# Doubling the third unit's inverse blocks for all chunks at once, inside the second unit's steps

## The chip, the cores and the metric

The kernel runs on one core of a Trainium2 chip. The metric is the device time of one execution in microseconds. TensorE does the matmuls, VectorE (DVE), ScalarE (ACT) and GpSimd (POOL) the elementwise work, and SyncE (SP) issues most DMAs. Each engine works through its own queue in order and waits for semaphores.

## The reference

Three layers follow each other. The first is linear attention with the delta rule, over 4 batches, 8 heads, 768 positions and 48 dimensions; the second is a gated layer, the third a choice of one of 8 experts for each token.

```python
for t in range(S):
    kt, vt, bt = (k_n[:, :, t], v[:, :, t], beta[:, :, t, None])
    y[:, :, t] = np.einsum('bhd,bhde->bhe', q[:, :, t], state)
    v_old = np.einsum('bhde,bhd->bhe', state, kt)
    state = state + bt[:, :, :, None] * np.einsum('bhd,bhe->bhde', kt, vt - v_old)
...
gate = 1.0 / (1.0 + np.exp(-(x @ w_gate)))
val = x @ w_val
return (gate * val @ w_out).astype(np.float32)
...
e_idx = np.argmax(logits, axis=1)
for e in range(E):
    mask = e_idx == e
    h = np.maximum(xc[mask] @ w1[e], 0.0)
    y[mask] = gate_w[mask, None] * (h @ w2[e])
out[do_compute] = xc + y
```

## The kernel before, in words

The 3072 tokens are cut into 12 units of 256 tokens, u = 0 to 11; the text calls u = 0 the first unit, u = 1 the second, u = 2 the third, u = 3 the fourth. A unit holds four chunks of 64 positions, one for each batch, with 8 heads each.

**Attention.** Inside a chunk the recurrence is a triangular system of 64 x 64 for each head. `gram` multiplies keys with keys and queries (TensorE), and ScalarE copies the products to g (lines 257 and 258) and to the masked query part kq (line 280, then a mask on GpSimd, line 281). From g comes the inverse tt of the system. There are two ways to it:
- The first three units (0 to 2) invert diagonal blocks of 16 on VectorE (`solve16`) and then double them twice with small matmuls: from 16 to 32 and from 32 to 64. That is `spread` (three VectorE instructions for each chunk) and `double` with its products ip, iy, jp and jy. The results of one product are copied by ScalarE or VectorE before the next.
- The units from the fourth on send g through DRAM (scr_g) to a block layout bt (`blocks`), and VectorE solves blocks of 32 in a long row of small instructions (`solve`): norms first (lines 324 to 336), then bt times a factor (340), 31 pairs of a product and a sum (351 and 356), a last product (358). The answer goes back through DRAM to tt, and `combine` finishes it with two products in the unit before its use.

`chain` carries the state through the chunks of a unit: ks at step 3, w at step 5 (it needs tt), y and s at step 7. It makes the input x of the next unit of the gated layer.

**Gated layer.** A unit has twelve steps f = 0 to 11, one for each 128 of the 1536 inner columns. In a step TensorE does the group gv_f (18 matmuls, `first`), ScalarE the sigmoid, VectorE the product sg_f, ScalarE its rounding gh_f and GpSimd the rest gl_f (`gate`); two steps later TensorE adds the step to the accumulators (`second`, lines 849 and 852). gv has two banks in PSUM, so gv_f waits until sg_(f-2) is done. From the second unit on the queues of TensorE, VectorE and ScalarE keep the order in which the program is written (`in_order`). The first unit (`block`) is left to a scheduler with priorities; there the weights are decoded too, and `fold` adds ten columns to each weight tile (transposes at line 775, products at line 781).

**Order around the change.** Behind the first unit the program writes `doubles()`, the third unit's doubling, chunk by chunk in pairs; its priority lets the scheduler put it into the first unit's tail. Then the second unit begins. In its step GRAMF = 0 it writes the fourth unit's grams and blocks and starts that unit's `solve`, a generator that yields an estimated time before each piece; `spend` runs pieces up to a budget for each step (the list SPEND). What is left of a solve when the next unit's grams come is run then. Routing of the unit before (`route`: copies of the accumulators at line 865, nine small VectorE instructions, a rank product) starts in step 0 of the second unit, in step 1 of the others.

The tile yc of the doubling lies in the same memory as the squares of `solve` (tag dn), so the squares wait for the last product jy.

Of the kernel before, what the change touches and what calls it, by code (L numbers as in the profile page):

```python
# [10 lines left out]
F32 = mybir.dt.float32  # L11
# [80 lines left out]
RANKF = 3  # L92
GRAMF = 0
LOADF = 8
LAG = 2
JOINF = 3
WHEN = {5: 1, 7: 4}
SPEND = 0, 0, 1.1, 2.8, 3.6, 4.0, 2.4, 1.2, 2.4, 2.4, 2.4, 2.4


class Kernel:
# [74 lines left out]
def sl(a, n):  # L176
    return slice(a, a + n)


class Attention:  # L180
# [295 lines left out]
    def double(self, u, c, pool, tag, bufs):  # L476

        k, nc = self.k, self.k.nc
        d = self.u[u]
        g, tt, yc, zc, gm = (d[x] for x in ("g", "tt", "yc", "zc", "gm"))  # L480
        s = sl(4 * c, 4)
        rc = d["rc"][:, s]
        quarters = [(pr, 4 * c + pr, slice(q, q + 32), (q, q)) for pr in range(4) for q in range(0, 128, 32)]

        def bank(n, w):
            return pool.tile([128, 4, w], F32, name=f"{n}{u}_{c}", tag=tag, bufs=bufs)

        ps = bank("ip", 16)
        for pr, n, q, at in quarters:
            nc.tensor.matmul(ps[q, pr], gm[q, n], yc[q, n, 16:32], start=True, stop=True, tile_position=at)  # L490
        yield
        nc.scalar.activation(rc, ps, AF.Copy, scale=-1.0)
        ps = bank("iy", 16)
        for pr, n, q, at in quarters:
            nc.tensor.matmul(ps[q, pr], zc[q, n], rc[q, pr], start=True, stop=True, tile_position=at)
        yield
        nc.vector.tensor_tensor(yc[:, s, 16:32], yc[:, s, 16:32], ps, op=ALU.add)
        for b in (1, 0):
            nc.vector.tensor_scalar(tt[:, c, :, sl(32 * b, 32)], yc[:, s], self.sel[:, 6 + b:7 + b], None, op0=ALU.mult)
        nc.vector.transpose(zc[:, s], yc[:, s])  # L500
        ps = bank("jp", 32)
        for pr in range(4):
            for p0 in (0, 64):
                nc.tensor.matmul(
                    ps[p0:p0 + 32, pr], g[p0 + 32:p0 + 64, c, pr, 0:32], tt[p0 + 32:p0 + 64, c, pr, 32:64],
                    start=True, stop=True, tile_position=(p0 + 32, p0))
        yield
        for p0 in (0, 64):
            nc.scalar.activation(yc[p0:p0 + 32, s], ps[p0:p0 + 32], AF.Copy, scale=-1.0)
        ps = bank("jy", 32)  # L510
        for pr in range(4):
            for p0 in (0, 64):
                nc.tensor.matmul(
                    ps[p0:p0 + 32, pr], zc[p0:p0 + 32, 4 * c + pr], yc[p0:p0 + 32, 4 * c + pr],
                    start=True, stop=True, tile_position=(p0, p0))
        yield
        for p0 in (0, 64):
            nc.scalar.activation(tt[p0:p0 + 32, c, :, 32:64], ps[p0:p0 + 32], AF.Copy)
        yield

    def lengthen(self, u, i):
# [726 lines left out]
def turns(*gens, fill={}):  # L1248

    n, more = 0, True  # L1250
    while more:
        more = [1 for g in gens if next(g, g) is not g]
        for f in fill.get(n, ()):
            f()
        n += 1


def program(ctx, tc, io, out):
# [219 lines left out]
        yield  # L1478
        yield from at.solve16(2, 0)

    def doubles():
        banks = (k.ps_a, "rw", 1), (k.ps_a, "y", 1)
        for cs in ((0, 1), (2, 3)):
            for c in cs:
                at.spread(2, c)
            turns(*[at.double(2, c, *banks[c % 2]) for c in cs])

    def between():

        tags = "prep", "rw", "y"  # L1490
# [73 lines left out]
        block()  # L1564
    dctx.close()
    m1.late = k.pool("late")
    with k.band("prep"):
        doubles()
    def spend(pieces, time):

        pieces[1] += time
        with k.band("solve"):
            while pieces[1] > 0:
                pieces[1] -= pieces[2]
                pieces[2] = next(pieces[0], 99)
# [6 lines left out]
    def second():  # L1582
        with k.band("second"):
            m1.second(*behind.popleft())
# [3 lines left out]
    with k.in_order(*engines[0:3]):  # L1588
        for u in range(1, NU):
            more = u + 1 < NU  # L1590
            if more:
                with k.band("top"):
                    xs[u + 1] = xp.tile([128, 2, KT3, UT], F32R, name=f"x{u + 1}", tag="x", bufs=2)
                chain = at.chain(u + 1, xs[u + 1], "prep")
            join = at.combine(u + 1) if 2 < u + 1 < NU else iter(())
            route = m1.route(u - 1)
            for f in range(NF):
                with k.band("main"):
                    fp = m1.first(u, f, xs[u])
                with k.band("gate"):  # L1600
                    g = m1.gate(*fp)
                    q = next(g)
                    drain(g)
                if f == RANKF:
                    with k.band("route"):
                        drain(route)
                if f == GRAMF:
                    spend(solve, 99)
                if f == GRAMF and u + 2 < NU:
                    with k.band("prep"):  # L1610
                        for c in range(CPU_):
                            at.gram(u + 2, c, (k.ps_a, ("prep", "y", "rw", "s")[c], 1))
                        at.blocks(u + 2)
                    solve = [at.solve(u + 2), 0, 1.1]
                if f == JOINF - 1:
                    with k.band("prep"):
                        next(join, None)
                spend(solve, SPEND[f])
                if more:
                    if f == JOINF:  # L1620
                        with k.band("prep"):
                            next(join, None)
                        with k.band("top"):
                            next(chain)
                    if f == JOINF + 1:
                        with k.band("prep"):
                            drain(join)
                    if f in WHEN:
                        with k.band("top"):
                            for _ in range(WHEN[f]):  # L1630
                                next(chain, None)
                    if f == LOADF and u + 3 < NU:
                        load(u + 3)
                    if f == LOADF and 2 < u + 2 < NU:
                        with k.band("prep"):
                            at.beside(u + 2)
                behind.append(q)
                if len(behind) > LAG:
                    second()
                if f == (LAG - 1 if u > 1 else 0):  # L1640
                    with k.band("route"):
                        next(route)
                        next(route)
            if u + 2 == NU:
                at.ctx.close()
                m2 = Moe2(k, m1)
        while behind:
            second()
# [114 lines left out]
```

## Time and profile before

| what | value |
|---|---|
| time, median of 3 runs | 975.41 us (975.26 to 978.01) |
| profiled execution | 984.58 us, of it span 982.8 us |
| TensorE busy | 890.0 us, 91% of the span |
| VectorE busy | 632.5 us, 64% |
| ScalarE busy | 426.1 us, 43% |
| GpSimd busy | 346.1 us, 35% |

The profile is of one execution, and its times count from the span's start. Busy time is the union of an engine's instructions; a line such as "203.54 5.39 PE ... x48" gives the start, the time that the instructions took together, and their number, and in brackets the idle time before them with what ended it. The granted clock is a share of 2.4 GHz: 1.00 is that level, 0.50 is 1.2 GHz, and a value between them is a mix of both in the stretch. In the trace gv_3 of the second unit starts at 216.31, its gv_5 at 225.05, and gv_0 of the third unit at 253.85.

### The profile page before, as it was taken

The numbers are of one execution on the slowest core, as the hardware profiler recorded it, in microseconds if no ns is written. First come the engines' busy times: TensorE is split into PE (matmuls) and PEld (weight loads), VectorE is DVE, ScalarE is ACT, GpSimd is POOL, SyncE is SP. The second block draws the span as 40 slices with busy tenths as digits, with TensorE's granted clock in tenths as the row PEclk, the third lists the DMA queues.
The fourth block names the chain that finished last, engine by engine and source line by source line (L and its number), as shares of the span: only waits on it lengthen the run. The fifth ranks groups of instructions, "written<-read, shape, count | busy, mean of one in ns | idle before, by whom it ended". The sixth has DMA issues, their size and how long they took to land.

```text
span 982.8 us, 26579 instructions
## 1 busy us (share of the span) xinstructions
PE 890.0 (91%) x10833; PEld 852.5 (87%) x10833; DVE 632.5 (64%) x1858; ACT 426.1 (43%) x998; POOL 346.1 (35%) x411
## 2 busy tenths in 40 slices
PE   6259887889999899999999999999989987999996
PEld 5247776789989899898989999898989987999996
DVE  6828886529586675858667575857721234877774
ACT  6365564452444425343442434343223233555553
POOL 6202662342533415253341514343222333231421
PEclk9998878879999999999999999999979999999999
DMA  8490304132313334331333433133020167766620
GB/s 194 143 382 24 76 2 124 31 71 66 82 38 80 94 74 98 78 70 38 85 94 74 98 80 97 40 67 80 10 55 15 34 216 257 223 229 201 222 83 14
DMA packets 132428, 99.29 MB, mean 101 GB/s; under 512 B 88231, under 2 KB 111868, under 8 KB 132304
## 3 DMA queue, kind: packets, MB, share of 16 engines
q1 hardware_dynamic: 125264, 78.44, 29.4%
q0 software_dynamic: 6624, 18.81, 6.4%
q8 instruction: 86, 1.41, 0.7%
q14 instruction: 38, 0.31, 0.1%
q10 hardware_dynamic: 416, 0.33, 0.1%
HBM read 76.66 MB, written 18.61 MB: 97 GB/s over the span
## 4 chain that ended last, share of the span: by engine, by line
PE 63%; DVE 17%; DMA 6%; ACT 5%; issue 5%; SPq 2%; POOL 1%; POOLq 0%; ACTq 0%; DVEq 0%
PE gv L826 24%; PE acc L849 9%; PE poe L1032 6%; PE he L1015 6%; PE acc L852 4%; PE gram L252 3%; PE w L664 2%; PE y L677 2%; DMA raw<-in_w 2%; DVE dec L756 2%; PE s L694 2%; DVE dec L757 1%; DVE sg L837 1%; PE m1p L559 1%; ACT tt L574 1%
## 5 line engine op out<-in xcount | busy, mean ns | idle before, releaser
L826 PE MATMUL gv<-x,w 128*128 128x256 f32 x2592 | 348.7, 289 | 2.2 <-ACT w L765 1.3
L826 PEld LDWEIGHTS gv<-x,w 128*128 128x128 f32 x2592 | 340.0, 196 | 4.2 <-ACT w L765 1.5
L840 POOL TENSOR_TENSOR gl<-sg,gh 128x256 fp32r<-128x256 f32 x144 | 117.1, 813 | 379.8 <-ACT gh L839 361.9
L837 DVE TENSOR_TENSOR sg<-sg,gv 128x256 f32<-128x256 f32 x144 | 60.1, 417 | 131.6 <-ACT sg L836 131.6
L849 PE MATMUL acc<-w,gh 128*128 128x394 f32 x576 | 140.1, 364 | 5.1 <-ACT w L783 3.6
L836 ACT ACTIVATE sg<-gv 128x256 f32<-128x256 f32 x144 | 54.9, 381 | 181.5 <-PE gv L826 178.5
L839 ACT ACTIVATE gh<-sg 128x256 fp32r<-128x256 f32 x144 | 60.2, 418 | 146.6 <-DVE sg L837 146.0
L849 PEld LDWEIGHTS acc<-w,gh 128*128 128x128 f32 x576 | 99.6, 195 | 9.8 <-ACT w L783 3.7
L351 DVE TENSOR_TENSOR tmp<-xx,bt 128x126 f32<-128x126 f32 (+28 forms) x299 | 91.9, 313 | 6.5
L356 DVE TENSOR_TENSOR xx<-xx,tmp 128x126 f32<-128x126 f32 (+28 forms) x299 | 88.3, 301 | 8.9
L281 POOL TENSOR_TENSOR kq<-kq,consts 64x256 f32<-64x256 f32 x96 | 72.9, 759 | 28.7 <-ACT kq L280 19.1
L852 PE MATMUL acc<-w,gl 128*128 128x394 f32 x288 | 78.4, 353 | 3.5 <-POOL gl L840 3.2
L934 DVE TENSOR_TENSOR w2le<-rawe,w2he 128x768 fp32r<-128x768 f32 x66 | 63.4, 962 | 10.1 <-ACT w2he L933 9.4
L252 PE MATMUL gram<-kq 48*64 48x128 f32 x768 | 56.6, 305 | 9.8 <-DMA kq<-in_kq 7.3
L252 PEld LDWEIGHTS gram<-kq 48*64 48x64 f32 x768 | 50.6, 153 | 13.7 <-DMA kq<-in_kq 6.0
L852 PEld LDWEIGHTS acc<-w,gl 128*128 128x128 f32 x288 | 54.9, 195 | 3.6 <-POOL gl L840 3.5
L933 ACT ACTIVATE w2he<-rawe 128x768 fp32r<-128x768 f32 x66 | 55.4, 840 | 2.0 <-DMA rawe<-in_w 1.9
L766 POOL TENSOR_TENSOR w<-dec,w 128x576 fp32r<-128x576 f32 x24 | 32.0, 1348 | 59.7 <-ACT w L765 48.1
L1015 PE MATMUL he<-x2he,w2he 128*128 128x256 f32 x168 | 48.3, 288 | 0.5 <-DVE hle L1024 0.5
L1015 PE MATMUL he<-x2le,w2he 128*128 128x256 f32 x168 | 47.3, 282 | 0.0
L1023 ACT ACTIVATE hhe<-he 128x256 fp32r<-128x256 f32 x64 | 24.5, 383 | 52.5 <-PE he L1015 52.4
L1015 PE MATMUL he<-x2he,w2le 128*128 128x256 f32 x168 | 47.1, 280 | 0.0
(330 smaller groups left out, 1553.5 us busy)
## 6 DMA issues: line engine op xcount, KB each, us to landing
rawe<-in_w SPq DMA_DIRECT2D x64, 384.0 KB, 4.8
raw<-in_w SPq DMA_DIRECT2D x24, 576.0 KB, 7.8
kq<-in_kq SPq DMA_DIRECT2D x44, 192.0 KB, 4.7
kv<-in_kv SPq DMA_DIRECT2D x22, 384.0 KB, 5.3
xa<-x POOLq DMA_DIRECT2D x12, 392.0 KB, 5.9
out<-x POOLq DMA_DIRECT2D x24, 192.0 KB, 4.1
bt<-scr_g SPq DMA_DIRECT2D x18, 256.0 KB, 4.9
xx<-in_eye SPq DMA_DIRECT2D x9, 256.0 KB, 5.4
```

Of the source, the lines that this page charges most:

```text
L252: self.last = nc.tensor.matmul(ps[o0:o0 + 64, pr], kt[r0:r0 + 48, cc, pr, :], kq[r0:r0 + 48, cc, pr, par:par + 2], start=True, stop=True).ins
L281: nc.gpsimd.tensor_tensor(q, q, mask[p], op=ALU.mult)
L351: v.tensor_tensor(t, x[:, :ni, m:m + 1].to_broadcast([128, ni, b - a]), bt[:, m:m + 1, m + 1 + a:m + 1 + b].to_broadcast([128, ni, b - a]) ...
L356: v.tensor_tensor(x[:, :ni, m + 1 + a:m + 1 + b], x[:, :ni, m + 1 + a:m + 1 + b], t, op=ALU.add)
L826: nc.tensor.matmul(gv[:, j], self.part(f, j, w)[:, c], y[:, a], start=n == 0, stop=n == 8)
L837: nc.vector.tensor_tensor(sg, sg, gv[:, 1], op=ALU.mult)
L839: nc.scalar.activation(gh, sg, AF.Copy)
L840: (nc.gpsimd if u < PG else nc.vector).tensor_tensor(gl, sg, gh, op=ALU.subtract)
L849: nc.tensor.matmul(self.acc[t], a[:, s], self.part(f, 2, b), start=f == 0 and n == 0, stop=False)
L852: nc.tensor.matmul(self.acc[t], gl[:, sl(128 * t, 128)], self.part(f, 2, 1), start=False, stop=f == NF - 1)
L934: nc.vector.tensor_tensor(l, raw, h, op=ALU.subtract)
L1015: nc.tensor.matmul(ps, ww[:, 0, s], xx[:, a], start=n == 0, stop=n == 8)
```

## The change

`doubles()` is gone. The third unit's doubling is written into the second unit's steps 1 to 4: in step 1 `spread_all` and the product ip, in step 2 iy, in step 3 jp, in step 4 jy, each for all four chunks in one bank, with the copies behind it merged. The products are as many as before. The fourth unit's grams, their blocks and the start of its solve go from step 0 to step 4 of the second unit, and its solve has a budget list of its own. From the third unit on nothing in the program text differs.

```diff
+GRAMF1 = 4
+DOUBLE2 = 1
 SPEND = 0, 0, 1.1, 2.8, 3.6, 4.0, 2.4, 1.2, 2.4, 2.4, 2.4, 2.4
+SPEND1 = 0, 0, 0, 0, 1.1, 3.6, 4.0, 4.0, 4.0, 2.8, 2.8, 2.8
...
+    def spread_all(self, u):
+
+        v = self.k.nc.vector
+        d = self.u[u]
+        for b in range(2):
+            v.tensor_tensor(
+                d["yc"][:, :, sl(16 * b, 16)], d["td"],
+                d[f"g{b}"].rearrange("p (n o) -> p n o", o=1).to_broadcast([128, 4 * CPU_, 16]), op=ALU.mult)
+        v.transpose(d["zc"], d["yc"])
+
+    def double_all(self, u, pool, tag, bufs):
...
+        def bank(n, w):
+            return pool.tile([128, 4 * CPU_, w], F32, name=f"{n}{u}", tag=tag, bufs=bufs)
+
+        ps = bank("ip", 16)
+        for n, q, at in quarters:
+            nc.tensor.matmul(ps[q, n], gm[q, n], yc[q, n, 16:32], start=True, stop=True, tile_position=at)
+        nc.scalar.activation(rc, ps, AF.Copy, scale=-1.0)
+        yield
+        ps = bank("iy", 16)
+        for n, q, at in quarters:
+            nc.tensor.matmul(ps[q, n], zc[q, n], rc[q, n], start=True, stop=True, tile_position=at)
+        nc.vector.tensor_tensor(yc[:, :, 16:32], yc[:, :, 16:32], ps, op=ALU.add)
+        for b in (1, 0):
+            nc.vector.tensor_scalar(tn[:, :, sl(32 * b, 32)], yc, self.sel[:, 6 + b:7 + b], None, op0=ALU.mult)
+        nc.vector.transpose(zc, yc)
+        yield
+        ps = bank("jp", 32)
...
+        for p0 in (0, 64):
+            nc.scalar.activation(yc[p0:p0 + 32], ps[p0:p0 + 32], AF.Copy, scale=-1.0)
+        yield
+        ps = bank("jy", 32)
...
+        for p0 in (0, 64):
+            nc.scalar.activation(tn[p0:p0 + 32, :, 32:64], ps[p0:p0 + 32], AF.Copy)
+        yield
...
-    with k.band("prep"):
-        doubles()
...
+            grams, budget = (GRAMF, SPEND) if u > 1 else (GRAMF1, SPEND1)
...
-                if f == GRAMF:
+                if f == grams:
                     spend(solve, 99)
-                if f == GRAMF and u + 2 < NU:
+                if f == grams and u + 2 < NU:
...
-                spend(solve, SPEND[f])
+                spend(solve, budget[f])
...
                 if len(behind) > LAG:
                     second()
+                if u == 1 and DOUBLE2 <= f < DOUBLE2 + 4:
+                    with k.band("prep"):
+                        if f == DOUBLE2:
+                            at.spread_all(2)
+                            double = at.double_all(2, k.ps_a, "prep", 1)
+                        next(double)
```

The order of the queues shows where this lands. First TensorE's queue from the first unit's last accumulating group on (acc with gh_11 and gl_11), before the change; jp and jy are the doubling of chunks 2 and 3, gram_1 to gram_3 the fourth unit's grams, gv_1 to gv_3 groups of the second unit.

```order
L849 MATMUL acc_0_1141<-w_2082,gh_11_2150 128x394
L849 MATMUL acc_1_1142<-w_2082,gh_11_2150 128x394
L852 MATMUL acc_0_1141<-w_2082,gl_11_2151 128x394
L852 MATMUL acc_1_1142<-w_2082,gl_11_2151 128x394
L504 MATMUL jp_2_2380<-tt_81,g_1220 32x32 x8
L504 MATMUL jp_3_2393<-tt_81,g_1220 32x32 x8
L513 MATMUL jy_2_2404<-early_y,early_z 32x32 x8
L513 MATMUL jy_3_2415<-early_y,early_z 32x32 x8
L252 MATMUL gram_1_2477<-kq_101 64x128 x8
L252 MATMUL gram_2_2492<-kq_105 64x128 x8
L252 MATMUL gram_3_2507<-kq_105 64x128 x8
L826 MATMUL gv_1_2554<-x_1583,w_850 128x256 x18
```

The same place of the same queue with the change; ip and iy are the doubling of all four chunks.

```order
L903 MATMUL acc_0_1141<-w_2082,gh_11_2150 128x394
L903 MATMUL acc_1_1142<-w_2082,gh_11_2150 128x394
L906 MATMUL acc_0_1141<-w_2082,gl_11_2151 128x394
L906 MATMUL acc_1_1142<-w_2082,gl_11_2151 128x394
L548 MATMUL ip_2256<-early_y,early_bt 32x16 x64
L880 MATMUL gv_2_2322<-x_1583,w_876 128x256 x18
L903 MATMUL acc_0_2348<-w_325,gh_0_2199 128x394 x2
L903 MATMUL acc_1_2349<-w_325,gh_0_2199 128x394 x2
L906 MATMUL acc_0_2348<-w_325,gl_0_2200 128x394
L906 MATMUL acc_1_2349<-w_325,gl_0_2200 128x394
L553 MATMUL iy_2356<-early_bt,early_z 32x16 x64
L880 MATMUL gv_3_2425<-x_1583,w_1181 128x256 x18
```

gv_1 has moved ahead into the tail, the grams are gone from here, and ip stands directly between the tail and gv_2. The next piece is VectorE's queue with the change, from the end of the first unit's routing (oh, ob) to the spread that ip needs and to sg_2.

```order
L937 TENSOR_TENSOR oh_2212<-eq_2211,mx_2210 128x16
L938 TENSOR_TENSOR oh_2212<-oh_2212,cm_2214 128x16
L939 CAST ob_2213<-oh_2212 128x16
L891 TENSOR_TENSOR sg_1_2246<-sg_1_2246,gv_1_2227 128x256
L529 TENSOR_TENSOR early_y<-early_bt,early_nt 128x16x16
L529 TENSOR_TENSOR early_y<-early_bt,early_w 128x16x16
L532 STREAM_TRANSPOSE early_z<-early_y 128x512
L891 TENSOR_TENSOR sg_2_2341<-sg_2_2341,gv_2_2322 128x256
```

The spreads (the two products into early_y) stood in the first unit before, around its sg_10, and stand behind the routing and sg_1 now. The last piece is ScalarE's queue with the change, from the last gram's copies in step 4 to the copies of w in step 5.

```order
L260 ACTIVATE g_2574<-gram_3_2620 64x256
L261 ACTIVATE g_2574<-gram_3_2620 64x256
L283 ACTIVATE kq_105<-gram_3_2620 64x4x64 x2
L327 ACTIVATE sq_0_2650<-kv_102 128x384
L327 ACTIVATE sq_1_2653<-kv_106 128x384
L572 ACTIVATE tt_81<-jy_2662 32x16x32 x2
L890 ACTIVATE sg_5_2716<-gv_5_2697 128x256
L893 ACTIVATE gh_5_2717<-sg_5_2716 128x256
L722 ACTIVATE sw_83<-w_0_2743 64x384
```

The copies of tt were ahead of the grams 1 to 3 and stand behind all grams' copies and behind the two squares now, and the sigmoid of step 5 behind them.

## Rows read from the trace of the kernel before

**Rows 1.** Busy time by stage: stretch, length, PE, PEld, DVE, ACT, POOL, clock, DMA.

```profile
183.20:197.50 14.30, 14.30 (x395) 13.04 (x395) 4.84 (x20) 6.59 (x23) 3.81 (x5) 1.00 0.01 3
197.50:208.86 11.36, 8.84 (x134) 7.74 (x133) 1.50 (x7) 6.46 (x20) 3.44 (x6) 0.75 0.01 2
208.86:216.31 7.45, 7.45 (x44) 7.45 (x43) 2.24 (x11) 3.47 (x10) 5.42 (x8) 0.69 0.69 127
216.31:225.05 8.74, 8.74 (x119) 8.62 (x118) 6.42 (x25) 2.54 (x6) 4.41 (x6) 1.00 0.25 91
220.99:252.48 31.49, 31.49 (x382) 30.92 (x381) 29.57 (x133) 7.79 (x21) 8.79 (x10) 1.00 0.26 59
```

**Rows 2.** Chain that ended last, in the first unit's tail: start, us, what.

```profile
187.35 2.13 PE gv L826 x18
190.11 0.77 PE wt L781 x6
193.40 0.48 PE wt L775 x3
193.87 0.71 PE acc L849 x4
194.58 0.36 PE acc L852 x2
194.94 0.66 PE ip L490 x54
```

**Rows 3.** Timeline of TensorE: fourth unit's grams, then fifth unit's: start, us, what.

```profile
203.54 5.39 PE L252 MATMUL gram<-kq 48*64 48x128 f32 x48 [2.00 <-ACT tt L518]
256.08 3.71 PE L252 MATMUL gram<-kq 48*64 48x128 f32 x64
```

**Rows 4.** Timeline of ScalarE and VectorE: first unit's routing, from its first to last instruction.

```profile
210.46 0.87 ACT L865 ACTIVATE x<-acc 128x394 f32<-128x394 f32 x2
212.78 0.17 DVE L885 CAST ob<-oh 128x16 bf16<-128x16 f32 x1
```

**Rows 5.** Groups by line and shape, VectorE, 218 to 256: busy us, mean ns, idle.

```profile
L837 DVE TENSOR_TENSOR sg<-sg,gv 128x256 f32<-128x256 f32 x9 | 3.7, 416 | 0.3 <-ACT sg L836 0.2
```

**Rows 6.** Timeline of TensorE: gv_3 and gv_5 of the second unit, gv_0 of the third.

```profile
216.31 2.29 PE L826 MATMUL gv<-x,w 128*128 128x256 f32 x18
225.05 2.28 PE L826 MATMUL gv<-x,w 128*128 128x256 f32 x18
253.85 2.29 PE L826 MATMUL gv<-x,w 128*128 128x256 f32 x18
```

**Rows 7.** Timeline of ScalarE: squares in the second unit; copies in the third.

```profile
217.76 0.53 ACT L324 ACTIVATE sq<-kv 128x384 f32<-128x384 f32 x1 [0.62 <-DVE nt L325]
262.73 0.38 ACT L258 ACTIVATE g<-gram 64x256 f32<-64x256 f32 x1
263.13 0.78 ACT L280 ACTIVATE kq<-gram 64x256 f32<-64x256 f32 x2
281.68 1.18 ACT L574 ACTIVATE tt<-x2p 32x512 f32<-32x512 f32 x2
```

**Rows 8.** The blocks' DMAs in the third unit: timeline of SP, then time to landing.

```profile
266.68 1.14 SPq L296 DMA_DIRECT2D bt<-scr_g  x2
DMA to landing us min/median/max: 3.7/4.1/4.6
```

**Rows 9.** Timeline of VectorE in the second unit: key products' subtraction, and sg_10.

```profile
225.97 1.01 DVE L655 TENSOR_TENSOR kv<-kv,ks 128x384 f32<-128x384 f32 x2
252.06 0.41 DVE L837 TENSOR_TENSOR sg<-sg,gv 128x256 f32<-128x256 f32 x1
```

**Rows 10.** A wait at w of a later unit, and the stretch behind it.

```profile
453.50 0.31 PE L664 MATMUL w<-kv,tt 64*64 64x48 f32 x2 [1.45 <-ACT tt L574]
455.70:459.20 3.50, 3.50 (x26) 3.41 (x22) 3.19 (x12) 2.37 (x5) 0.77 (x1) 0.51 0.00 0
```

**Rows 11.** Copies of jy to tt, all doublings: ns min, median, max, first and last start.

```profile
L518 ACT ACTIVATE tt<-jy x24: 250/268/271, 58.5 to 203.2; 32x128 f32<-32x128 f32 x24
```

More of the change, by code (lines that the diff above doesn't have):

```diff
@@ L518, in double @@
             nc.scalar.activation(tt[p0:p0 + 32, c, :, 32:64], ps[p0:p0 + 32], AF.Copy)
+        yield
[8 more added lines that the diff above has]
+    def double_all(self, u, pool, tag, bufs):
+        k, nc = self.k, self.k.nc
+        d = self.u[u]
+        g, tt, yc, zc, gm, rc = (d[x] for x in ("g", "tt", "yc", "zc", "gm", "rc"))
+        quarters = [(n, slice(q, q + 32), (q, q)) for n in range(4 * CPU_) for q in range(0, 128, 32)]
+        halves = [(n, *divmod(n, 4), p0) for n in range(4 * CPU_) for p0 in (0, 64)]
+        tn = tt.rearrange("p c h t -> p (c h) t")
+        def bank(n, w):
[14 more added lines that the diff above has]
+        ps = bank("jp", 32)
+        for n, c, pr, p0 in halves:
+            nc.tensor.matmul(
+                ps[p0:p0 + 32, n], g[p0 + 32:p0 + 64, c, pr, 0:32], tt[p0 + 32:p0 + 64, c, pr, 32:64],
+                start=True, stop=True, tile_position=(p0 + 32, p0))
+        for p0 in (0, 64):
+            nc.scalar.activation(yc[p0:p0 + 32], ps[p0:p0 + 32], AF.Copy, scale=-1.0)
+        yield
+        ps = bank("jy", 32)
+        for n, c, pr, p0 in halves:
+            nc.tensor.matmul(
+                ps[p0:p0 + 32, n], zc[p0:p0 + 32, n], yc[p0:p0 + 32, n], start=True, stop=True, tile_position=(p0, p0))
+        for p0 in (0, 64):
+            nc.scalar.activation(tn[p0:p0 + 32, :, 32:64], ps[p0:p0 + 32], AF.Copy)
@@ L1479, in third @@
         yield from at.solve16(2, 0)
[L1481 to L1486, printed above, removed]
     def between():
```

## The prediction

> **What bounds the kernel now.** I read the busy time by stages first [rows 1]. TensorE is busy in every microsecond of the second unit: the stretch from 216.31 to 225.05 has 8.74 of 8.74 us, and 220.99 to 252.48 has 31.49 of 31.49. In that last stretch VectorE has 29.57 of 31.49, so it is full to 94% beside a full TensorE and has 1.9 us to spare. The second place to see is the tail of the first unit: from 197.50 to 208.86 TensorE has only 8.84 of 11.36 us, and its granted clock is 0.75, then 0.69 up to 216.31. The timeline of that place shows why: the doubling's last copies hold the next grams back for 2.00 us, and 48 gram matmuls then take 5.39 us where 64 take 3.71 us at full clock [rows 3]. So the change takes work out of a stage with gaps and a low clock, and puts it into a stage without gaps.
>
> **The change part by part.** I walk along TensorE's queue of the changed kernel, put the durations of the trace on it, and compare one point after the other. Both kernels have the same queue up to 183.2. Matmul groups are f, as in gv_f, of the second unit unless I say otherwise.
>
> *The tail.* Between 183.2 and the end of the first unit TensorE now has three groups gv (gv_11 of the first unit, gv_0 and gv_1 of the second), three fold products, two fold transposes and three pairs of accumulating groups: 3 x 2.13 + 3 x 0.77 + 2 x 0.48 + 3 x (0.71 + 0.36) = 12.9 us [rows 2]. Twice it waits for a fold's copy, for which I allow 0.4 us each as an estimate. So the last accumulating group ends near 197.0. gv_1, the doubling and the grams stood between here and gv_2 before.
>
> *The new wait at ip.* The next matmul, ip, needs the spread on VectorE. On VectorE the spread stands behind the routing of the first unit, and that needs the accumulators' copies on ScalarE. In the trace the copies begin at 210.46 and the routing's last cast ends at 212.95, 2.5 us in all [rows 4]. Behind them come sg_1 and two spreads of 128 x 256, each taken as the product of that shape, 0.42 us [rows 5]: 1.25 us. With 0.3 us for the hand-overs ip starts about 4.0 us after the last group, at 201.0. gv_2 stands behind ip and waits too. Then ip 0.66, gv_2 2.13, the accumulating group 1.07 and iy 0.66 [rows 2] bring gv_3 to 205.6. Before it started at 216.31 [rows 6]: a lead of 10.7 us.
>
> *Moved work, paid again.* From gv_3 to gv_5 TensorE needed 8.74 us [rows 1, 6]. Now jp and jy (as ip at most, 0.66 each) and the 64 grams (3.71) come on top, so gv_5 starts at 219.4 instead of 225.05. Lead 5.7 us. Their evacuations on VectorE (the add, two selections and a transpose) lie beside gv_3 and the key products: VectorE was 6.42 busy of 8.74 there and gives up its squares' reductions and the scaling, so I cost them at nothing; if that cover were gone they would cost 2 to 3 us.
>
> *The new wait at w.* The second unit's step 5 multiplies with tt of the third unit, whose last copies now stand on ScalarE behind the grams' copies and the two squares. In the third unit the trace has that very row of copies: gv_0 ends at 256.14 (253.85 + 2.29) and the last masked copy at 263.91, 7.8 us later; two squares with the wait between them take 1.7, and two copies of tt 1.18 [rows 6, 7]. So tt is ready 10.7 us after gv_4's end, which is at 214.1: 224.8. TensorE is through with grams, accumulating group, jy and gv_5 at 221.6. It waits 3.2 us. Lead 2.5 us.
>
> *The late blocks.* VectorE's solve for the fourth unit begins with the blocks bt, which travel by DMA through DRAM from the grams' copies. In the third unit the last copy of g ends at 263.11, the two DMAs are issued between 266.68 and 267.82 and land 3.7 to 4.6 us after issue: near 271.7, or 15.6 us after the gv before the grams ended [rows 7, 8]. In the second unit of before these grams stood three steps ahead of the solve; now one step lies between. bt lands at 214.1 + 15.6 = 229.7. VectorE is through with sg_5 near 225.6, and everything behind it in its queue, sg_6 too, stands still for 4 us.
>
> *The solve against the gates.* From the first instruction on bt (220.99) to the end of sg_10 (252.48) VectorE needed 31.5 us [rows 1, 9]. Now sg_4, sg_5 and the two subtractions of the key products come earlier: minus 2 x 0.42 and 1.01 [rows 5, 9], and minus half a microsecond of idle time that it had, leaves 29.2 us. gv_0 of the third unit needs the bank that sg_10 frees, so it starts at 229.7 + 29.2 = 258.9. Before it started at 253.85 [rows 6]. TensorE's own work would have let it start near 251, so it waits some 7 to 8 us in steps 8 to 12. The lead of 2.5 us has become a lag of 5.0 us.
>
> *After that.* The fourth unit's solve ends about 1.4 us later, seen from gv_0 of the third unit, than it did; the gates and copies of that place are late by as much, and TensorE had waits in this unit already. Price between 0 and 1.4 us; I take 0.7. No later unit changes.
>
> *The clock.* A wait of 1.45 us at w in a later unit is followed by a stretch of 3.5 us at a granted clock of 0.51 [rows 10], a loss of 0.49 x 3.5 = 1.7 us; the low stretch of before, 11.36 us at 0.75 and 7.45 at 0.69, lost 0.25 x 11.36 + 0.31 x 7.45 = 5.2 us [rows 1], and that is already in the numbers of before. The new wait of 4.0 us at ip is longer than either wait, and dense work follows it. I take one short stretch, 1.7 us, between 0 and 5.2. The later waits may bring low stretches as well, but those lie beside VectorE's 29 us and cost nothing more. The Trainium skill (TensorE: Matmul & The Clock Gate, What's actually happening) says that the throttled clock is the default and only activity releases it, so that idle stretches bring it back, and the trace agrees where the 0.51 stands behind a wait [rows 10]; by that rule the stretch after ip falls to the low level and the sum is the one below. Were the clock to stay up there, the sum would be 1.7 us less.
>
> *Sum.* 5.0 + 0.7 + 1.7 = 7.4 us slower. The profiled execution took 984.58 us, 982.8 of it span, so it would take 992. The timed runs' median is 975.41, some 9 us shorter; I carry the same difference over: 982.8 us. Ends of the unknowns: clock 0 to 5.2, third unit 0 to 1.4, blocks and hand-overs 1.5 either way, VectorE's 29.2 us 2 either way. Not all fall on one side; the likeliest case's own range is 979 to 987.
>
> **Rivals.**
> *Faster: VectorE keeps up.* TensorE's lead at gv_5 is 5.7 us. If the solve's list up to sg_10 took 24 us instead of 29.2, gv_0 of the third unit would start where it did; from there each microsecond less is a gain, down to the waits at ip and w, which leave at most 2.5 us without the clock's loss and 5.7 without the wait at w. That would be 969.7 to 973. For it speaks that the merged instructions are cheaper: eight copies of tt at 0.268 [rows 11] become two at 0.59 [rows 7]. Against it: the saved instructions lie in stages where neither VectorE nor ScalarE sets the end, and the solve's own instructions are not changed. The Trainium skill (VectorE: DVE Perf Modes, The TRN2 errata) holds that instructions that read SBUF pay a fixed latency each, so that large tiles pay it once; by it the doubling's merging is a plain gain, and this rival's; the two rows on tt agree in kind (four times the elements in 2.2 times the time), though they read PSUM. Chance 0.12.
> *No change.* The blocks land before VectorE asks for them, as when the DMAs are issued right behind the copies (4 us saved), and the clock stays up: 5.0 - 4.0 + 0 to 0.7, within 2 us of 975.4. The trace speaks against it: the issue waited 3.6 us behind the last copy in the third unit. Chance 0.17.
> *Slower still.* The wait at ip brings a low stretch as long as that of before and the third unit pays its 1.4 us: 975.4 + 5.0 + 5.2 + 1.4 = 987. Chance 0.08.
> That the move doesn't happen is out: the order shows the doubling behind the tail and the grams behind gv_4.
>
> **How the numbers follow.** The forecast has 0.63. A run differs from no change here by over 0.3%, 2.9 us, or can't be told from it. Faster 0.12, same 0.17, slower 0.63 + 0.08 = 0.71. The range goes from 974.5, inside the case of no change, to 987: it leaves out most of the faster case and a little above.
>
> **What would show it.** In the profile after: a TensorE wait of about 4 us at ip (line 548) and 3 us at w (line 718); VectorE idle about 4 us ahead of the copy at line 332; TensorE waits of 7 us in all for sg between gv_9 and gv_0 of the third unit; that gv_0 start 4 to 7 us later than 253.85; the third to twelfth units unchanged in length. The prediction is wrong if the blocks land within 11 us of gv_4's end, or if TensorE has no waits behind gv_8.

## The result, and the profile after

The change makes the kernel slower: 987.61 us (median of 4 runs, 985.80 to 989.32) against 975.34 us of before on the same chip; ratio 1.0124, 95% interval 1.0091 to 1.0158, so 12.3 us. The forecast was 982.8 with a range to 987.0: the direction and the mechanism came, but 7.4 us of loss were forecast where 12.3 came, and the time lies 0.6 us above the range.

Times count from the span's start, and executions differ by some us before the place of the change is reached. So I compare from a **mark**: the start of the last four matmuls of gv_10 of the first unit, up to which all kernels here have the same queue on TensorE. (The expectations below call it "the last group of gv_11"; it is that of gv_10.) The mark is at 180.57 in the profile of before shown above, at 180.47 after:

```profile
180.57 0.72 PE L826 MATMUL gv<-x,w 128*128 128x256 f32 x4
180.47 0.71 PE L880 MATMUL gv<-x,w 128*128 128x256 f32 x4
```

First TensorE's timeline after, from the first unit's tail to gv_0 of the third unit: start, us, what, and in brackets the idle time before it.

```profile
195.51 0.52 PE L906 MATMUL acc<-w,gl 128*128 128x394 f32 x2
199.48 1.90 PE L548 MATMUL ip<-early_y,early_bt 32*32 32x16 f32 x128 [3.45 <-DVE early_y L529]
201.32 3.44 PE L880 MATMUL gv<-x,w 128*128 128x256 f32 x18
...
205.75 1.26 PE L553 MATMUL iy<-early_bt,early_z 32*32 32x16 f32 x128
206.94 2.40 PE L880 MATMUL gv<-x,w 128*128 128x256 f32 x18
...
212.67 0.94 PE L561 MATMUL jp<-tt,g 32*32 32x32 f32 x47
214.08 0.28 PE L561 MATMUL jp<-tt,g 32*32 32x32 f32 x6 [0.47 <-issue]
214.85 0.39 PE L561 MATMUL jp<-tt,g 32*32 32x32 f32 x11 [0.49 <-issue]
215.16 2.38 PE L880 MATMUL gv<-x,w 128*128 128x256 f32 x18
217.47 3.71 PE L255 MATMUL gram<-kq 48*64 48x128 f32 x64
...
222.38 1.20 PE L569 MATMUL jy<-early_y,early_z 32*32 32x32 f32 x64
223.51 2.39 PE L880 MATMUL gv<-x,w 128*128 128x256 f32 x18
227.38 0.31 PE L718 MATMUL w<-kv,tt 64*64 64x48 f32 x2 [1.48 <-ACT tt L572]
...
253.82 4.21 PE L880 MATMUL gv<-x,w 128*128 128x256 f32 x18 [5.52 <-DVE sg L891]
...
262.47 2.40 PE L880 MATMUL gv<-x,w 128*128 128x256 f32 x18
```

The wait at ip is there (3.45 us), and behind it ip and gv_2 are slow: gv_2 takes 3.44 us where gv_3 takes 2.40. The grams start 37.0 us after the mark. gv_10 waits 5.52 us for the bank that VectorE frees, and gv_0 of the third unit starts 82.0 us after the mark; in [rows 6] it was 253.85 - 180.57 = 73.3.

VectorE and SyncE after, on the way between: the blocks' copy with its idle time; then SyncE's issues; then the stages of both engines by windows (PE, PEld, DVE, ACT, POOL, clock, DMA).

```profile
233.29 0.19 DVE L332 COPY nt<-bt 128x32 f32<-128x32 f32 x1 [4.48 <-DMA bt<-scr_g]
262.01 0.41 DVE L891 TENSOR_TENSOR sg<-sg,gv 128x256 f32<-128x256 f32 x1
...
224.12 1.93 SPq L270 DMA_DIRECT2D scr_g<-g  x4
227.69 2.46 SPq L299 DMA_DIRECT2D bt<-scr_g  x2
```

```profile
196.03:206.94 10.91, 7.46 (x281) 7.17 (x280) 3.46 (x14) 2.63 (x7) 3.69 (x5) 0.69 0.27 74
206.94:223.51 16.57, 15.62 (x317) 14.40 (x309) 5.09 (x15) 7.15 (x18) 6.50 (x9) 1.00 0.02 3
233.29:262.42 29.13, 23.61 (x256) 22.64 (x254) 27.15 (x127) 4.46 (x13) 4.65 (x6) 0.88 0.28 63
253.82:258.00 4.18, 4.18 (x19) 4.18 (x20) 4.18 (x28) 0.67 (x2) 0.75 (x1) 0.50 0.19 42
```

The blocks land 15.8 us after gv_4's end (217.47 to 233.29), VectorE has stood still for 4.48 us, and from there to the end of sg_10 it is busy 27.15 of 29.13 us while TensorE has 23.61: this stretch is VectorE's. TensorE's low clock in it (0.50 from 253.82 on) costs nothing more, since gv_0 starts 0.05 us after sg_10 ends. All that stood in the chain of the forecast, with 15.6 and 29.2 us. That 29.2 came out so exactly has a reason: up to step 10 the two budget lists add up to the same (22.3 us of estimated time), and in both traces the same pieces of the solve stand ahead of sg_10.

### The profile page after: what moved, and what is told of

Same layout as the page of the kernel before. It is cut to its first block, busy times and chain, and to the rows that moved or that the text cites. A ratio compares the mean times of both kernels' runs of the same rounds, so it can differ in the third digit from the quotient of the medians.

```text
span 984.0 us, 26533 instructions
## 1 busy us (share of the span) xinstructions
PE 888.5 (90%) x10833; PEld 848.4 (86%) x10833; DVE 627.4 (64%) x1837; ACT 423.2 (43%) x983; POOL 345.1 (35%) x411
## 4 chain that ended last, share of the span: by engine, by line
PE 58%; DVE 19%; ACT 8%; DMA 7%; issue 5%; SPq 2%; POOL 1%; ACTq 0%; POOLq 0%; DVEq 0%
PE gv L880 21%; PE acc L903 8%; PE poe L1086 7%; PE he L1069 6%; PE acc L906 4%; PE y L731 2%; DMA raw<-in_w 2%; PE w L718 2%; ACT kq L283 2%; DVE dec L810 2%; DVE sg L891 1%; DMA tt<-scr_t 1%; PE s L748 1%; PE m1p L613 1%; PE gram L255 1%
## 5 line engine op out<-in xcount | busy, mean ns | idle before, releaser
L255 PE MATMUL gram<-kq 48*64 48x128 f32 x768 | 54.0, 296 | 8.3 <-DMA kq<-in_kq 7.8
L255 PEld LDWEIGHTS gram<-kq 48*64 48x64 f32 x768 | 48.3, 148 | 12.1 <-DMA kq<-in_kq 7.1
L1077 ACT ACTIVATE hhe<-he 128x256 fp32r<-128x256 f32 x64 | 24.5, 383 | 53.1 <-PE he L1069 40.4
```

What stands on the lines that cost most here:

```text
L255: self.last = nc.tensor.matmul(ps[o0:o0 + 64, pr], kt[r0:r0 + 48, cc, pr, :], kq[r0:r0 + 48, cc, pr, par:par + 2], start=True, stop=True).ins
```

## Experiments

The theory to be tested (theory 1 in the expectations): from ip to the third unit there is one chain. What makes TensorE late for the fourth unit's grams is handed on through the copies, DRAM and VectorE's solve to the third unit. Its rivals: VectorE's list sets the gates wherever TensorE stands (theory 2), or the granted clock behind the new waits is the whole loss (theory 3).

All kernels in one table, us from the mark, in the profiled execution: start of the (last) fourth unit's grams, of VectorE's copy of bt, of gv_0 and of m1p of the third unit; last the median's difference to before on the same chip.

| kernel | grams | bt | gv_0 | bt to gv_0 | m1p | time |
|---|---|---|---|---|---|---|
| before, first profile | 23.0 | 40.4 | 73.3 | 32.9 | 89.1 | |
| before, second profile (again) | 22.4 | 38.7 | 70.8 | 32.1 | 86.7 | 0 |
| after | 37.0 | 52.8 | 82.0 | 29.2 | 98.4 | +12.3 |
| ahead | 36.8 | 52.1 | 81.3 | 29.3 | 97.7 | +10.6 |
| gfirst | 37.1 | 49.4 | 78.8 | 29.4 | 95.2 | +11.1 |
| late_grams | 32.1 | 47.4 | 76.6 | 29.2 | 93.0 | +6.1 |
| late1 | 23.6 | 38.4 | 70.7 | 32.3 | 86.6 | +1.0 |
| late2 | 27.4 | 44.5 | 74.1 | 29.6 | 90.1 | +5.7 |
| merged_tail | 18.1 | 35.1 | 67.3 | 32.2 | 83.2 | -1.2 |
| merged5 (same kernel) | 18.8 | 35.9 | 68.1 | 32.2 | 83.9 | -0.7 |
| early_g | 31.0 | 49.1 | 81.5 | 32.5 | 97.4 | +12.9 |
| lean | 40.0 | 55.4 | 77.9 | 22.5 | 102.6 | +14.3 |
| lean_g | 38.1 | 50.8 | 75.2 | 24.4 | 99.8 | +14.0 |
| filled | 40.9 | 57.3 | 86.5 | 29.2 | 102.9 | +16.0 |

**again**: the kernel before, unchanged.

> The kernel before, unchanged, for a second profile: the first one was an execution of 984.58 us where the timed runs gave 975. Expected 973 to 978 us, gv_0 of the third unit at 253.9 us as in the first profile, and the 7 to 9 us of difference in low-clock stretches of later units (units of 55.7 us where the first profile has 59.7, 57.3 and 57.2).

976.40 us. TensorE's timeline of this profile at the place of [rows 3, 6]:

```profile
205.47 4.50 PE L252 MATMUL gram<-kq 48*64 48x128 f32 x48 [2.00 <-ACT tt L518]
...
253.90 2.30 PE L826 MATMUL gv<-x,w 128*128 128x256 f32 x18
```

The mark is at 183.08 here, so gv_0 comes 70.8 us after it, 2.5 earlier than in the first profile: the 48 grams take 4.50 us instead of 5.39 and the low stretch behind them is shorter. The 7 to 9 us of difference lie with low-clock stretches as expected (the third to ninth units take 55.64 to 56.24 us each from grams to grams, the first profile has 59.70, 57.34 and 57.15 among them), but 2.5 of it lie at the very place that the change replaces. That gv_0 starts at 253.90 in both is chance.

**ahead**: the spread goes into the tail.

```diff
+    with k.band("prep"):
+        at.spread_all(2)
...
                         if f == DOUBLE2:
-                            at.spread_all(2)
                             double = at.double_all(2, k.ps_a, "prep", 1)
```

> The change with the spread written into the first unit's tail, ahead of the routing, so that ip finds it done; all else as in the change. Theory 1 (everything from ip to the third unit is one chain: TensorE's time of arrival at the fourth unit's grams is handed on one for one through the grams' copies, the DMAs through DRAM and VectorE's solve to gv_0 of the third unit): the wait of 3.45 us at ip and the slow ip and gv_2 behind it (1.9 us) go, grams at 212 to 213 instead of 217.5, gv_0 of the third unit at 257 to 258 instead of 262.5, time 982 to 983. Theory 2 (VectorE is full and its list alone sets the gates, wherever TensorE stands): gv_0 stays at 262, time 987. Theory 3 (what is lost is the granted clock behind the new waits): 1.9 us less, 985.5.

986.49 us, ratio 1.0104 (1.0088 to 1.0121). A miss: the grams came at 36.8, not at 32. ip no longer waits, but its copy stands on ScalarE behind the routing's copies of the accumulators and behind a gh whose sg stands behind the routing on VectorE, and iy, the next product, waits:

```profile
206.13 1.80 PE L553 MATMUL iy<-early_bt,early_z 32*32 32x16 f32 x128 [1.62 <-ACT early_bt L549]
207.87 4.21 PE L880 MATMUL gv<-x,w 128*128 128x256 f32 x18
```

The scheduler had also put the last accumulating groups behind ip and gv_2, so the routing started later. The wait was moved, and the low clock with it (gv_3 4.21 us). From the grams on the chain holds: 29.3 us from bt to gv_0.

**gfirst**: the grams' copies to g ahead of those to kq.

```diff
-                        for c in range(CPU_):
-                            at.gram(u + 2, c, ...)
+                        held = [at.gram(u + 2, c, ..., hold=u == 1) for c in range(CPU_)]
+                        if u == 1:
+                            for c in range(CPU_):
+                                at.keep(u + 2, c, held[c])
```

> The change with ScalarE's copies of the fourth unit's grams in another order: all eight copies to g ahead of the eight to kq, so that the DMAs to DRAM start 2.4 us earlier. TensorE's queue is as in the change. Theory 1 (late blocks): bt lands near 230.9 instead of 233.3, VectorE idles 2.1 us ahead of the copy of bt instead of 4.5, gv_0 of the third unit starts 2.4 us earlier, time 985. Theories 2 and 3 (VectorE's list alone, or the clock alone): no difference, 987 to 988.

986.97 us, ratio 1.0112 (1.0084 to 1.0141). At gv_0 theory 1 is right and theory 2 is wrong: TensorE comes to the grams at the same time (37.1), bt 3.4 us earlier, gv_0 3.2 us earlier. In the time 0.6 to 1.2 us of that are left, less than the runs' spread; by the time alone (987 to 988 expected of theories 2 and 3) the run would have gone the other way.

**late_grams**: the doubling stays in the tail as before, the grams go to step 4.

```diff
+    with k.band("prep"):
+        doubles()
...
-                if u == 1 and DOUBLE2 <= f < DOUBLE2 + 4:
...
```

> Only half of the change: the doubling stays in the first unit's tail, chunk by chunk as before, and the fourth unit's grams, blocks and solve go to the second unit's step 4 with the new budget list. Theory 1: TensorE comes to the grams near 212 to 213, so the blocks still land late (near 229) and gv_0 of the third unit starts at 258, 4 us later than before: 980 to 982. If the merged doubling with its waits at ip and jp is the whole loss, this kernel takes what before took, 975, or less, since the tail has no grams.

981.94 us, ratio 1.0073 (1.0046 to 1.0099): 6.1 us, at gv_0 5.8. Half of the loss, with no new wait ahead of the solve. The largest of TensorE's waits from 183 to 330 us (us in total, times, longest), and two groups gv, gv_10 and gv_0 of the third unit:

```profile
PE gv L880 <- DVE sg L891: 8.5, 4, 5.9
...
248.27 3.67 PE L880 MATMUL gv<-x,w 128*128 128x256 f32 x18 [5.89 <-DVE sg L891]
...
256.93 2.39 PE L880 MATMUL gv<-x,w 128*128 128x256 f32 x18 [0.52 <-DVE sg L891]
```

TensorE is ahead of everything and still waits 8.5 us for VectorE, which got its blocks late. gv_10 runs partly at the low clock behind its wait, but gv_0 waits 0.52 us for VectorE once more, so that low clock costs nothing here. The other 5.4 us at gv_0 (82.0 - 76.6) are the doubling's new place.

**late1, late2**: the same with the grams in step 1 and in step 2, each with a list of its own. late1 has that of the later units, so step and list change together; late2 has it one step later. The edit of late1:

```diff
-GRAMF1 = 4
+GRAMF1 = 1
-SPEND1 = 0, 0, 0, 0, 1.1, 3.6, 4.0, 4.0, 4.0, 2.8, 2.8, 2.8
+SPEND1 = 0, 0, 1.1, 2.8, 3.6, 4.0, 2.4, 1.2, 2.4, 2.4, 2.4, 2.4
```

> The half with the late grams again (doubling in the tail, chunk by chunk, as before), but the fourth unit's grams in step 1 of the second unit instead of step 4, with the budget list of the later units. Law of theory 1, from the runs so far: bt lands 15.3 us after the grams' start, and gv_0 of the third unit starts 29 to 31 us after that, unless TensorE is later by itself. Here the grams come some 10 us earlier than with step 4, bt lands 38 us after the last group of gv_11 in the first unit's tail (47.4 with step 4, 38.7 in the second profile of before), so gv_0 of the third unit comes 1 to 2 us earlier than before: 973 to 975. If not the grams' lateness but their move out of the tail costs the time, it stays near 982.

> The same with the grams in step 2 and the later units' budget list one step later. By the law of theory 1 one step later is 3.3 us later: bt at 41, gv_0 of the third unit 1 us later than before, 976 to 978. If the loss with step 4 came from the denser budget list of its steps 5 to 8, and not from the lateness, this kernel takes 975 as before.

late1 979.62 us, ratio 1.0009 (0.9988 to 1.0031); late2 984.32 us, ratio 1.0059 (1.0031 to 1.0086). With step 1 the grams come at 23.6, nearly where before has them although gv_1 has gone ahead of them, and the loss is gone. gv_0 came at 70.7 as before, not 1 to 2 us earlier: TensorE has no wait for sg left, so it is its own work that ends there. late2 missed its 976 to 978 and is no clean point of the series: in its profile the grams' 48 matmuls wait 3.43 us for copies of tt, and a low stretch follows. Its 5.7 us are not explained by lateness of the blocks alone.

**merged_tail and merged5**: the merged doubling in the tail, grams in step 0; the same kernel twice.

```diff
+    with k.band("prep"):
+        at.spread_all(2)
+        drain(at.double_all(2, k.ps_a, "rw", 1))
...
-            grams, budget = (GRAMF, SPEND) if u > 1 else (GRAMF1, SPEND1)
+            grams, budget = GRAMF, SPEND
```

> Only the other half of the change: the doubling for all chunks at once, but in the first unit's tail where it was, with the grams in step 0 as before. Theory 1: merging itself costs nothing and takes the wait of 2.00 us ahead of grams 1 to 3 away, since the copies of tt are done earlier; the low clock behind that wait goes too (1.7 us in the second profile of before): 970 to 973. If the merged products themselves are the loss (a chain of four products and copies that can't overlap), the tail becomes longer and the time is 976 to 980.

> The useful half again, with more rounds: doubling for all chunks at once in the first unit's tail, grams in step 0 as before. Its profile had gv_0 of the third unit 3.5 us earlier than the second profile of before, and then more low-clock stretches of 1.7 us each in later units (five against two), so that the time was 1.2 us less, within the interval. If those stretches fall by chance, the gain at gv_0 should show in the median: 2 to 3.5 us less than before, ratio 0.9965 to 0.998. If they belong to this kernel, the ratio is 0.998 to 1.001.

977.35 us, ratio 0.9993 (0.9971 to 1.0015), and 975.15 us, ratio 0.9991 (0.9974 to 1.0009): no difference that can be told. merged_tail missed its 970 to 973, merged5 came out as the second of its two cases. In the profiles the wait of 2.00 us [rows 3] is gone and gv_0 comes 2.8 to 3.5 us earlier than in the second profile of before. This kernel also gives the true price of the products at full clock (merged5):

```profile
186.05 1.26 PE L548 MATMUL ip<-early_y,early_bt 32*32 32x16 f32 x128
189.88 1.26 PE L553 MATMUL iy<-early_bt,early_z 32*32 32x16 f32 x128
194.03 1.20 PE L561 MATMUL jp<-tt,g 32*32 32x32 f32 x64
197.10 1.20 PE L569 MATMUL jy<-early_y,early_z 32*32 32x32 f32 x64
```

**early_g**: the spread ahead, ip in step 0, grams in step 3, copies to g first, and a budget list one step earlier.

```diff
-GRAMF1 = 4
-DOUBLE2 = 1
+GRAMF1 = 3
+DOUBLE2 = 0
...
```

> The whole change with its three delays taken out: spread ahead of the routing, ip at the end of step 0 (its copy on ScalarE then stands ahead of the routing's copies, which held it in the run with the spread ahead), everything one step earlier with the grams in step 3, and the copies to g ahead of those to kq. Theory 1: grams near 28 us after the last group of gv_11 instead of 37.0, bt 13 us later at 41, gv_0 of the third unit within 1 us of before: 975 to 978. If the work in the second unit is too much for TensorE or VectorE wherever it stands, 982 or more.

991.46 us, ratio 1.0126 (1.0093 to 1.0160). A miss, by new waits: the grams came at 31.0 instead of 28, and grams 1 to 3 wait 1.47 us for the routing's last VectorE instruction (base), ks of the same step 3.29 us for the copies to kq, which now come last and hold its banks (ks has those of grams 2 and 3), and jy behind it starts 9 us after the grams' end. The squares of the solve use the same memory as yc, so they wait for jy; the blocks had landed before VectorE could use them.

```profile
PE ks L706 <- ACT kq L285: 3.3, 1, 3.3
PE gram L255 <- DVE base L956: 1.5, 1, 1.5
```

**lean and lean_g**: a thinner budget list; lean_g has the copies to g first as well.

```diff
-SPEND1 = 0, 0, 0, 0, 1.1, 3.6, 4.0, 4.0, 4.0, 2.8, 2.8, 2.8
+SPEND1 = 0, 0, 0, 0, 1.1, 2.4, 2.4, 2.4, 2.4, 2.4, 2.4, 2.4
```

> The change with a thinner budget list for the second unit (2.4 in each of the steps 5 to 11 instead of 3.6, 4, 4, 4, 2.8, 2.8, 2.8): of the 102 multiply and add instructions of the solve, 50 instead of 94 stand ahead of sg_10 on VectorE, the rest goes behind it and into the third unit's step 0. TensorE's and ScalarE's queues and the blocks are as in the change. Theory 1 with the list as its last link (in four kernels so far gv_0 of the third unit came 29.2 to 29.4 us after bt): 44 instructions of 0.28 us less ahead of sg_10, so TensorE's wait of 5.5 us before gv_10 and the low clock behind it go (7.4 us); the solve ends as late as before, so the third unit's m1p waits about 3 us for tt: 982 to 984. If the gates wait for something else than the solve's list (the blocks themselves, or TensorE's own lateness), 987 to 988 stays.

> The same with the copies to g ahead of those to kq as well, so that bt lands 3.4 us earlier. By theory 1 TensorE itself is the bound up to gv_0 of the third unit now, and the solve ends 3 us earlier, so the wait at m1p goes: 979 to 982. If the two cures act on different things, or on nothing, the time is that of the kernel with the thinner list alone.

990.16 us, ratio 1.0161 (1.0135 to 1.0188), and 989.79 us, ratio 1.0162 (1.0135 to 1.0189). Both are misses: no faster than the change, and its interval (1.0091 to 1.0158) overlaps theirs, so they can't be called slower either. The gates behave as expected: from bt to gv_0 22.5 us instead of 29.2, in lean_g no wait for sg at all, gv_0 at 75.2. But the solve now ends later, and the third unit needs its result. TensorE, VectorE and GpSimd of lean_g there; the second line of VectorE is one of the solve's last small sums, the line of GpSimd the mask on the next grams:

```profile
271.92 1.68 PE L905 MATMUL acc<-w,gh 128*128 128x394 f32 x4 [3.00 <-ACT x L921]
281.02 1.92 PE L615 MATMUL m1p<-dn,g 32*32 32x32 f32 x64 [2.95 <-DVE dn L609]
...
263.66 0.23 DVE L361 TENSOR_TENSOR xx<-xx,tmp 128x70 f32<-128x70 f32 x1
264.60 0.78 DVE L361 TENSOR_TENSOR xx<-xx,tmp 128x56 f32<-128x56 f32 x1
...
269.61 1.09 DVE L363 TENSOR_TENSOR xx<-xx,w 128x512 f32<-128x512 f32 x1
280.52 0.77 DVE L609 STREAM_TRANSPOSE dn<-tt 128x256 f32<-128x256 f32 x2 [6.41 <-DMA tt<-scr_t]
...
263.69 6.46 POOL L286 TENSOR_TENSOR kq<-kq,consts 64x256 f32<-64x256 f32 x8 [0.43 <-ACT kq L285]
```

The same sum in the change, without GpSimd beside it:

```profile
262.58 0.22 DVE L359 TENSOR_TENSOR xx<-xx,tmp 128x56 f32<-128x56 f32 x1
```

The last product of the solve ends at 270.70, the answer comes back from DRAM 9.8 us later, and m1p is at 99.8 from the mark, later than in the change (98.4). The two cures did not act on one thing: I had looked at the gates, and with the gates relieved the end of the solve counts.

That end comes 38.7 us after bt here, in the change 32.1, and 3.8 of the 6.6 us lie in the last four pairs and the product: the thinner list leaves more behind sg_10, so these now run beside GpSimd's mask, where a sum takes 0.78 us that takes 0.22 in the change. Counted one by one over the whole trace of the change, none of the solve's 474 products and sums with no GpSimd instruction beside them took over 0.31 us, while 69 of the 124 beside one took 0.65 to 0.86. No run tests this by itself.

In lean the grams also came at 40.0 instead of 37.0, with TensorE's queue as in the change but more low clock ahead of them, so 3 us of its m1p are not the list's doing. This corrects theory 1: the chain's last link is m1p of the third unit. In the change m1p itself doesn't wait, the gates hold it; in lean and lean_g it waits for the solve, 3.85 and 2.95 us. The table's column of m1p less 86.7 follows the time's column, with a largest difference of 2.6 us (gfirst).

**filled**: 26 matmuls on constants ahead of ip.

```diff
         ps = bank("ip", 16)
+        for _ in range(26):
+            nc.tensor.matmul(
+                ps.rearrange("p a b -> p (a b)"), k.cb[:, 0:128], k.cb[:, 0:1].to_broadcast([128, 256]),
+                start=True, stop=True)
```

> The change with 26 matmuls of 128 x 256 on constants written ahead of ip into ip's bank (0.125 us each by the profile's row of such matmuls, 3.25 us in all), which fill TensorE's wait of 3.45 us at ip; their results are overwritten. This parts the clock's share from the wait's. Theory 1 with the clock as one link of the chain: the granted clock stays at 1.00 through ip and gv_2 (ip 1.26 us and gv_2 2.40 as at full clock, instead of 1.90 and 3.44), the fourth unit's grams come 1.7 us earlier, 35.3 instead of 37.0 us after the last group of gv_11, gv_0 of the third unit 1.7 us earlier; time 985 to 986.5. Theory 3 (the clock is the whole loss): about 980. If the low clock behind the wait has nothing to do with TensorE's idle time, ip and gv_2 stay slow and the time is 987 to 988.

989.75 us, ratio 1.0168 (1.0129 to 1.0208). As a test of the clock it is inconclusive. The scheduler put the 26 matmuls ahead of the last accumulating groups, so the routing came 3 us later and ip waited as before:

```profile
199.18 3.06 PE L548 MATMUL ip<-consts_b 128*128 128x256 bf16 x26
202.00 0.61 PE L907 MATMUL acc<-w,gh 128*128 128x394 f32 x2
202.44 0.52 PE L910 MATMUL acc<-w,gl 128*128 128x394 f32 x2
206.31 1.62 PE L552 MATMUL ip<-early_y,early_bt 32*32 32x16 f32 x128 [3.35 <-DVE early_y L529]
```

For theory 1 it is a test by accident, and a weak one: 3.06 us put in front of the chain came out as 3.7 us in the time (16.0 against 12.3), with 29.2 us from bt to gv_0 again. But the two intervals overlap, and in this profile a low stretch behind the mark takes 1.4 us more than in the change, which are part of the 40.9.

## Why the prediction was right in kind and too small

- *The wait at ip*: predicted 4.0 us, 3.45 came, by the mechanism named. ip started 19.0 us after the mark instead of 20.4.
- *The late blocks and the solve against the gates*: predicted 15.6 us from gv_4's end to bt, 4 us of idle VectorE, 29.2 us from bt to gv_0; measured 15.8, 4.48, 29.2. Five kernels with this budget list gave 29.2 to 29.4. The waits in steps 8 to 12 were predicted as 7 us in all; 5.52 came, in one place.
- *The new wait at w*: predicted 3.2, measured 1.48 and 0.30. Behind gv_4's end TensorE took 8.4 us to gv_5's end instead of 7.5, and the first copy of tt came 9.9 us after it instead of 10.7, so the wait was shorter. It decided nothing, since VectorE's list ended later.
- *The step that failed first* is the size of the moved products: "jp and jy (as ip at most, 0.66 each)", and ip and iy at 0.66. That row [rows 2] holds 54 records and is the product of two chunks. All four chunks are 128 records, 1.26 us at full clock; jp and jy are 1.20. The three products ahead of the grams were priced 1.7 us too low (2 x 0.60 + 0.54). jp also had gaps of 0.47 and 0.49 us in which TensorE waited for nothing that the profile shows. With the low clock in ip and gv_2 (0.64 and 1.04 us over full clock) and ip's earlier start (1.4 us) that makes 3.0 of the 3.5 us by which the grams came later (37.0 instead of 33.5); the rest I didn't place. Of these 3.5 us the forecast had 1.7 in its clock term, so 1.8 us were missing.
- *The second failure* is the base: "I carry the same difference over". The first profile of before was 9 us slower than the median, and I took that surplus to lie outside the place of the change, while 2.5 us of it were the long low stretch of the tail, which I counted as removed by the change. An execution of the usual length has less of it, as far as one profile shows (again). Against the second profile gv_0 lags 11.2 us, not 8.7.
- *After that*: the third unit, from grams to grams, took 56.07 us instead of 55.65; 0.4 for the predicted 0.7.
- *Sum*: 2.5 + 1.8 + 0.2 (from gv_4's end to gv_0) - 0.3 = 4.2 of the 4.9 us between 7.4 and 12.3. The other 0.7 is within the spread of the runs.
- *The clock*: the row of gv_2 and that of 253.82 show the low level behind both long waits (3.45 and 5.52 us); the first cost ip and gv_2 1.7 us, as forecast, the second nothing, as argued. The Trainium skill (TensorE: Matmul & The Clock Gate, What's actually happening) says that the low clock is the default and that activity releases it; these two rows agree. That the clock is the whole loss is ruled out by late_grams, which loses 6.1 us, has no wait at ip and no slow gv_2, and hides its own low stretch in VectorE's time. How much of the rest filling the wait would give back is not shown, since that run missed its place.
- *The rival "slower still"* gave 987 at a chance of 0.08, the nearest number to the measured 987.6, but not by what came: it wanted 5.2 us from the clock behind ip, where 1.7 came, and 1.4 us in the third unit, where 0.4 came.
- *The faster rival* (VectorE keeps up) is refuted for the change. With the merging alone gv_0 is 2.8 to 3.5 us earlier in both profiles, but the time isn't shorter by a measurable amount. By the Trainium skill (VectorE: DVE Perf Modes, The TRN2 errata), which the prediction cites for this rival, instructions that read SBUF pay a fixed latency each, so that merging them is a gain. The profiles agree in kind at gv_0; whether that latency is the reason, or only the wait of 2.00 us that is gone, no run here shows. Both profiles have four stretches of low clock between 260 and 660 us, the first profile of before has three, the second one. Whether those belong to the kernel or fall by chance stays open.

No kernel here beats before beyond its interval; the merged doubling in the tail is level with it.

## What to carry to other kernels

Work that begins a chain over other engines and DRAM is priced by when it starts, not by how long it takes: follow it past the first gate to its last consumer (here from the gates gv_10 and gv_0 on to m1p of the next unit), or a cure at the gate only moves the wait on. Take a price from a row only after counting how many instructions the row holds and how many the moved step issues. Where the profiled execution is slower than the median, find out first how much of the surplus lies in the stretch that the change replaces.

## What the runs showed of the hardware

What a wait costs in clock was not the same from place to place. The wait of 1.45 us at w in before has a stretch of 3.5 us at 0.51 behind it [rows 10]; the wait of 1.48 us at w in the change has none (granted clock 1.00 from 227 to 251 us). Nor was all of the lost clock paid for: in the change it was low by 3.4 us of full clock from 196 us on, of which ip and gv_2 paid 1.7 and TensorE's wait took most of the rest, and by 3.4 from 251 on, which VectorE's time covered.

Two profiles of the unchanged kernel differed by 8.2 us in their spans (982.8 and 974.6), with low stretches at different places: between 260 and 700 us from 340, 456, 568 and 681 in the first, from 391 alone in the second.

The solve's small instructions on VectorE never took over 0.31 us in the change where no GpSimd instruction ran beside them, and 0.65 to 0.86 us in 69 of 124 cases where one did; what in GpSimd's work does it is not shown.
